# Linear-attention and MLP layers on one core: layer 1 started with ten TensorE-transposed tiles, another load order, biases by rows, and six sums off VectorE

## The chip, the cores and the metric

The kernel runs on one NeuronCore of a Trainium2 chip. Its engines work side by side, each through its own instruction queue in order: TensorE (PE in the profile, with its weight loads as PEld), VectorE (DVE), ScalarE (ACT), GpSimd (POOL) and SyncE (SP), which here only issues DMAs. The metric is the device time of one execution in microseconds; lower is better. What is reported is the median of several executions.

## The reference

Four layers act in turn on x, 2048 tokens by 576 channels, in bfloat16: A, B, A, B with the same weights for both A and both B.

```
x = x + A(layernorm(x));  x = x + B(layernorm(x));  x = x + A(layernorm(x));  x = x + B(layernorm(x))

A(x): q, k, v = x @ wqkv, 32 heads of 18;  phi(t) = where(t > 0, t + 1, exp(t)) + 1e-6
      kv = phi(k)^T v  and  z = sum phi(k), over all tokens
      o  = phi(q) kv / (phi(q) z + 1e-6);   return o @ wo
B(x): y = layernorm(x);  h = gelu_tanh(y @ w1 + b1), 4608 wide;  return h @ w2 + b2
```

Linear attention needs kv, the sum over all tokens, before any output of the layer; so layer A has two passes over the tokens.

## The kernel before

Tokens are cut into 16 tiles of 128. Everything stays on chip: x in `x_sb`, its normalised transpose in `yT` (channels on partitions, 5 blocks of 128 with the last one half filled), and all weights, each loaded once.

**Layer A, first pass** (`layer_A`, the loop at line 375). For each tile: `k_proj` (10 matmuls into two `k_ps` banks, exp on ScalarE, then phi finished on VectorE into `pk`), `v_proj` (10 matmuls, copied to `v_ring` by ScalarE), `kv_acc` of the tile before (5 matmuls that add to `kvacc`), and from tile 4 on one `q_proj` (`q_next`), which makes phi(q) for one group of heads and 512 tokens. There are 20 of these. **Second pass** (line 432): `num_stage` (5 matmuls, reciprocal and product on VectorE into a `y_ring` buffer, and a DMA transpose into `yT`, line 411) runs three tiles ahead of `wo_stage` (10 matmuls, and the residual sum). The residual sum of a tile is one VectorE instruction (line 305), but for tiles 4 to 7 it is a ScalarE copy (line 302) and a GpSimd sum (line 303). What is left of the 20 `q_proj` goes in between. After tiles 8, 10, 12 and 14 one group of the next MLP's first block is put in (`m1_group`, 36 matmuls), out of nine groups.

**The norm of a tile** (`Norm`) is four steps: statistics on VectorE (lines 211 to 220), the power -1/2 on GpSimd (line 225), the scaling on one of three engines (lines 236 and 240), and the transpose: either a DMA transpose issued by SyncE (line 249), or five TensorE transposes (line 253) and one copy of all five by ScalarE (line 255). In layer 1 the tiles 0 to 5 are transposed by TensorE, 6 to 15 by DMA; tiles 0 and 1 are scaled on VectorE and the others on GpSimd. Norms for later layers go through `Queue`: each `tick` lets every tile in it take its next step. In the second pass of layer A the first four tiles are fed to it for the MLP, scaled on ScalarE, their 64 tail channels doubled by GpSimd (line 244), and transposed by DMA.

**Layer B** (`LayerB`) takes blocks of 512 tokens: `m1_group` fills hT with gelu, then 72 matmuls for each tile and the residual sum. The lines 484 and 493 are its gelu and a one-column copy that orders its matmuls.

**What sets the order.** TensorE's order is written out: each matmul and transpose is chained to the one before (`pe`, line 122). The first loads are chained too (`chained`), all on SyncE's queue. The other engines get their order from a scheduler that runs when the kernel is built, by its own estimate of when things are ready; on the chip each engine keeps that order, so an instruction that waits holds back all behind it.

The loads of layer 1 are issued as follows: x tiles 0 and 1, k weights, x 2 and 3, v weights, x 4 and 5, then ten DMAs for the q weights, then two x tiles at the start of each tile of the first pass, and from tile 2 on one item of `late_pieces` in each: `wo`, nine pieces of `w1` (each with two small DMAs for its last 64 rows, `w1_tail`), the biases, and twelve pieces of `w2`. The bias b1 is read element by element into 128 partitions by 36 columns (`b1_raw`, line 171) and cast into `b1T` on VectorE (line 589).

Of the kernel before, what the change touches and what calls it, by code (L numbers as in the profile page):

```python
# [16 lines left out]
P = 128  # L17
NT = S // P
KD = 5
# [17 lines left out]
def build(tc, A_x, A_wqkv, A_wo, B_w1, B_b1, B_w2, B_b2, out, n_layers=4):  # L37
    nc = tc.nc
    with ExitStack() as ctx:
# [19 lines left out]
        def one(name):  # L59
            return ps_one.tile([P, 512], F32, name=name, tag="one")  # L60

# [80 lines left out]
        def load_wq(k):  # L142
            rows = P if k < 4 else 64
            src = A_wqkv[k * P:k * P + rows, :]
            chained(nc.sync.dma_start(out=wq_sb[0:rows, k, 0:4, 0:126],
                                      in_=src[:, 0:504].rearrange("p (g c) -> p g c", g=4)))
            chained(nc.sync.dma_start(out=wq_sb[0:rows, k, 4, 0:72], in_=src[:, 504:576]))
# [5 lines left out]
        def piece_w1(i):  # L153
            cs = slice(i * 512, (i + 1) * 512)
            chained(nc.sync.dma_start(out=w1_sb[:, 0:4, cs], in_=B_w1[0:4 * P, cs].rearrange("(k p) n -> p k n", p=P)))
            ts = slice(i * 256, (i + 1) * 256)
            for par in range(2):
                chained(nc.sync.dma_start(
                    out=w1_tail[64 * par:64 * (par + 1), ts].rearrange("k (f p) -> k f p", p=P),
                    in_=B_w1[4 * P:D, cs].rearrange("k (f two p) -> k f two p", two=2, p=P)[:, :, par, :]))  # L160
# [7 lines left out]
        def piece_biases():  # L168
            b1_raw = work.tile([P, NF], BF16, name="b1_raw", bufs=1)
            with nc.allow_non_contiguous_dma(reason="tiny one-time bias transpose load"):  # L170
                chained(nc.sync.dma_start(out=b1_raw[:], in_=B_b1.rearrange("(f p) -> p f", p=P)))
            bias_stage["b1"] = b1_raw
            chained(nc.sync.dma_start(out=b2_bc[:], in_=B_b2.partition_broadcast(P)))

# [28 lines left out]
        class Norm:  # L203
# [42 lines left out]
            def transposed(self):  # L246
# [3 lines left out]
                else:  # L250
                    tp = ps_one.tile([P, KD, P], BF16, name="tp", tag="one")
# [7 lines left out]
        class Queue:  # L259
# [3 lines left out]
            def feed(self, t, kind, eng="dve"):  # L263
                n = Norm(t, kind, eng, "dma")
# [44 lines left out]
        def layer_A(li, next_kind, before_tile, transposes, mlp):  # L309
# [65 lines left out]
            for t in range(NT):  # L375
                before_tile(t)
                k_proj(t)
                if t + 2 in transposes:
                    transposes[t + 2]()
# [3 lines left out]
                if t >= 4:  # L383
                    q_next()
            q_next()
# [263 lines left out]
```

## Time and profile before

| | us |
|---|---|
| median of 3 executions | 797.74 (797.67 to 798.62) |
| the profiled execution, its own time | 798.14 |
| its span, first to last instruction | 796.4 |
| TensorE busy in it | 765.2 |
| VectorE / ScalarE / GpSimd busy | 222.7 / 302.5 / 132.8 |
| mean granted TensorE clock | 0.987 |

A matmul row of the profile reads: line, engine, operation, what it writes and reads, shapes, count, and in brackets how long the engine had stood idle before it and who released it. All matmuls have line 129, the helper `mm`, so they are told apart by the tile they write: `k_ps`, `v_ps`, `kvacc`, `q_ps`, `num_ps`, `wo_ps` for layer A, `h_ps`, `hp_ps` and `m_ps` for layer B; `tp` (line 253) is the transpose. In the chain of waits a matmul's duration is its share of the pipelined stream, in the timeline it runs to its modelled end, so the latter is longer. "PEclk" is the TensorE clock that was granted, as a share of full speed.

### The profile page before, as it was taken

To read this page: it belongs to the slowest core of one execution; us is meant where nothing else is said; L and a number is where in the kernel's file an instruction comes from. 1 tells how busy PE (TensorE), PEld (TensorE's weight loads), DVE (VectorE), ACT (ScalarE), POOL (GpSimd) and SP (SyncE) were. 2 spreads that over 40 slices of the span, in tenths; PEclk is the share of its full clock that TensorE was granted. 3 is DMA by queue.
4 is the path that set the end of the run, shared out by engine and by line. 5 is a ranking of instruction groups with operands and counts; after the bars stand their busy time and mean duration, and the time that the engine had idled before them with its cause. 6 is when DMAs were issued, how large, how long until landed. Compare 5 with 4: busy or idle time off the path is not lost.

```text
span 796.4 us, 15153 instructions
## 1 busy us (share of the span) xinstructions
PE 765.2 (96%) x6416; PEld 488.8 (61%) x6416; DVE 222.7 (28%) x672; ACT 302.5 (38%) x638; POOL 132.8 (17%) x181
## 2 busy tenths in 40 slices
PE   7897979999999999999999996999999999999998
PEld 4675545477467547745787754546754774675476
DVE  6643884023103301300244576840000000000000
ACT  3464643600740461065036663343047016404610
POOL 7960060012102200200100004320100110010000
PEclk9998999999999999999999998999999999999999
DMA  8799153001300200100000015430000000000000
GB/s 212 187 206 274 39 104 59 2 9 17 43 1 17 51 2 9 17 10 1 18 17 1 1 34 93 84 58 8 16 9 1 16 16 1 2 23 9 2 8 23
DMA packets 86932, 33.88 MB, mean 43 GB/s; under 512 B 71696, under 2 KB 86864, under 8 KB 86864
## 3 DMA queue, kind: packets, MB, share of 16 engines
q1 hardware_dynamic: 86864, 32.91, 19.2%
q8 instruction: 50, 0.82, 0.4%
q14 instruction: 18, 0.15, 0.1%
HBM read 15.79 MB, written 2.36 MB: 23 GB/s over the span
## 4 chain that ended last, share of the span: by engine, by line
PE 83%; DVE 5%; POOL 4%; DMA 3%; issue 2%; ACT 1%; SPq 1%; POOLq 0%; DVEq 0%; ACTq 0%
PE m_ps L129 36%; PE h_ps L129 19%; PE hp_ps L129 15%; PE v_ps L129 4%; PE k_ps L129 4%; PE q_ps L129 3%; POOL y_ring L240 3%; DMA yT<-y_ring 2%; PE wo_ps L129 2%; DVE y_ring L408 1%; POOL ln_rstd L225 1%; PE kvacc L129 1%; DVE ln_st L211 1%; DMA b_raw<-in_B_b_dram 1%; DVE x_sb L305 1%
## 5 line engine op out<-in xcount | busy, mean ns | idle before, releaser
L129 PE MATMUL m_ps<-w_sb,hT 128*128 128x288 bf16 x2304 | 283.6, 286 | 0.0
L129 PEld LDWEIGHTS <-hT 128*128 128x128 bf16 x2304 | 224.8, 98 | 59.8 <-issue 3.4
L129 PEld LDWEIGHTS <-w_sb 64*128 64x128 bf16 x2304 | 123.9, 94 | 138.6 <-issue 4.6
L129 PE MATMUL hp_ps<-yT,w_sb 64*128 64x512 bf16 x1152 | 176.8, 376 | 0.8 <-DVE x_sb L305 0.8
L305 DVE TENSOR_TENSOR x_sb<-m_ps,xo 128x576 bf16<-128x576 f32 x32 | 24.2, 758 | 457.1 <-PE m_ps L129 457.1
L129 PE MATMUL h_ps<-yT,w_sb 64*128 64x512 bf16 x1152 | 149.2, 376 | 0.6 <-DVE y_ring L408 0.6
L493 ACT COPY relay_sb<-relay_sb 128x1 f32<-128x1 f32 x144 | 28.4, 197 | 283.2 <-PE h_ps L129 238.5
L129 PEld LDWEIGHTS <-yT 128*128 128x128 bf16 x960 | 94.1, 101 | 50.2 <-issue 10.7
L295 POOL TENSOR_TENSOR xo<-x_sb,b_bc 128x576 f32<-128x576 bf16 x32 | 40.8, 1274 | 456.1 <-DVE x_sb L305 455.8
L484 ACT ACTIVATE hT<-h_ps,b1T 128x512 bf16<-128x512 f32 x144 | 91.2, 684 | 44.5 <-PE h_ps L129 44.5
L484 ACT ACTIVATE hT<-hp_ps,b1T 128x512 bf16<-128x512 f32 x144 | 91.2, 693 | 0.0
L225 POOL TENSOR_TENSOR ln_rstd<-ln_u,neg_half 128x1 f32<-128x1 f32 x64 | 35.1, 552 | 148.9 <-DVE ln_u L220 127.4
L129 PE MATMUL wo_ps<-wo_sb,yT 128*128 128x288 bf16 x320 | 47.4, 298 | 9.4 <-DMA yT<-y_ring 9.2
L211 DVE BATCH_NORM_STATS2 ln_st<-x_sb 128x6 f32<-128x288 bf16 x128 | 52.3, 439 | 7.3 <-DMA x_sb<-in_A_x_dram 6.7
L129 PE MATMUL h_ps<-yT,w_tail 64*128 64x512 bf16 x144 | 54.1, 376 | 0.0
L129 PE MATMUL hp_ps<-yT,w_tail 64*128 64x512 bf16 x144 | 54.1, 376 | 0.0
L129 PE MATMUL k_ps<-wkv_sb,yT 128*128 128x288 bf16 x320 | 45.9, 290 | 8.0 <-DVE pk L328 7.7
L129 PE MATMUL q_ps<-yT,wq_sb 128*128 128x512 bf16 x200 | 50.3, 386 | 1.4 <-DVE y_ring L408 1.4
L129 PE MATMUL v_ps<-wkv_sb,yT 128*128 128x288 bf16 x320 | 47.6, 299 | 0.0
L323 ACT ACTIVATE phi_e<-k_ps 128x288 bf16<-128x288 f32 x64 | 24.4, 418 | 45.1 <-PE k_ps L129 42.1
L129 PEld LDWEIGHTS <-w_tail 64*128 64x128 bf16 x288 | 27.1, 94 | 17.1
L363 ACT ACTIVATE phi_e<-q_ps 128x512 bf16<-128x512 f32 x40 | 23.8, 596 | 26.8 <-PE q_ps L129 24.5
(59 smaller groups left out, 378.9 us busy)
## 6 DMA issues: line engine op xcount, KB each, us to landing
w_sb<-in_B_w_dram SPq DMA_DIRECT2D x12, 432.0 KB, 8.7
w_sb<-in_B_w_dram SPq DMA_DIRECT2D x9, 512.0 KB, 4.6
x_sb<-in_A_x_dram SPq DMA_DIRECT2D x16, 144.0 KB, 3.4
out_dram<-x_sb SPq DMA_DIRECT2D x16, 144.0 KB, 1.8
yT<-y_ring SPq DMA_TRANSPOSE x90, 2.6
wkv_sb<-in_A_wqkv_dram SPq DMA_DIRECT2D x2, 576.0 KB, 5.6
wo_sb<-in_A_wo_dram SPq DMA_DIRECT2D x1, 576.0 KB, 6.1
w_tail<-in_B_w_dram SPq DMA_DIRECT2D x18, 32.0 KB, 4.0
```

Source lines behind the costliest of these rows:

```text
L129: return pe(nc.tensor.matmul(out_, lhsT=lhsT, rhs=rhs, start=start, stop=stop, **kw))
L211: ins = nc.vector.bn_stats(out=stt[:, h, :], in_=xt[:, h * HALF:(h + 1) * HALF])
L225: nc.gpsimd.tensor_tensor(out=self.r[:], in0=self.u[:], in1=neg_half[:], op=ALU.pow)
L240: ins = eng.tensor_scalar(out=y[:, 0:D], in0=xt, scalar1=self.mv[:, 0:1], scalar2=self.r[:, 0:1], op0=ALU.subtract, op1=ALU.mult)
L295: nc.gpsimd.tensor_tensor(out=xo[:], in0=x_sb[:, t, :], in1=b2_bc[:], op=ALU.add)
L305: nc.vector.tensor_tensor(out=two(x_sb[:, t, :]), in0=halves, in1=two(xo), op=ALU.add)
L323: nc.scalar.activation(out=e[:, cols], in_=kp[:, 0:HALF], func=ACT.Exp)
L363: last["exp"] = nc.scalar.activation(out=e[:, 0:CA], in_=qp[:], func=ACT.Exp).ins.name
L408: nc.vector.tensor_tensor(out=o[:, h0 * DH:h1 * DH].rearrange("p (h c) -> p h c", c=DH), in0=nd[:, :, 0:DH], in1=rden[:, h0:h1].unsqueeze( ...
L484: last["gelu"] = nc.scalar.activation(out=hT[f][:, 0:CB], in_=dst[n], func=ACT.Gelu_apprx_tanh, bias=b1T[:, f:f + 1], scale=1.0).ins.name
L493: relay = nc.scalar.copy(out=relay_sb[:, 1:2], in_=relay_sb[:, 0:1])
```

## The change

1. Layer 1: the tiles transposed by TensorE are 0 to 9 (`TE = 10`), not 0 to 5; tile 2 is scaled on VectorE too; the transposes of tile t+2 stand at the end of tile t in TensorE's order, not between its k and v matmuls.
2. x tiles 6 to 9 are loaded ahead of the q weights and 10 to 15 right behind them; the q weights take seven DMAs, not ten.
3. `w1_tail` is loaded by two DMAs, not eighteen. The last four tiles of the first pass issue up to four late pieces each, so that all are issued there.
4. b1 is loaded as 36 rows of 128, transposed by TensorE after the last tile's `q_next`, and cast from PSUM.
5. The first `q_proj` stands at tile 3 in layer 1 and at tile 2 in layer 3, not at tile 4.
6. In both layers A the four tiles normalised for the MLP are transposed by TensorE and copied by ScalarE.
7. The residual sums of tiles 4 to 9, not 4 to 7, go by ScalarE and GpSimd.
8. The gelu table is loaded after tile 3 of the second pass, not 5, and MLP groups are put in after tiles 7, 9, 11, 13 and 15: five of them, not four.

```diff
@@ -59,6 +59,9 @@
         def one(name):
             return ps_one.tile([P, 512], F32, name=name, tag="one")
 
+        def one_bf16(name, shape):
+            return ps_one.tile(shape, BF16, name=name, tag="one")
+
 
         ident = const.tile([P, P], BF16, name="ident")
         nc.gpsimd.memset(ident[:], 0.0)
@@ -139,12 +142,14 @@
                                       in_=A_wqkv[0:4 * P, src].rearrange("(k p) n -> p k n", p=P)))
             chained(nc.sync.dma_start(out=wkv_sb[0:64, 4, dst], in_=A_wqkv[4 * P:D, src]))
 
-        def load_wq(k):
-            rows = P if k < 4 else 64
-            src = A_wqkv[k * P:k * P + rows, :]
-            chained(nc.sync.dma_start(out=wq_sb[0:rows, k, 0:4, 0:126],
-                                      in_=src[:, 0:504].rearrange("p (g c) -> p g c", g=4)))
-            chained(nc.sync.dma_start(out=wq_sb[0:rows, k, 4, 0:72], in_=src[:, 504:576]))
+        def load_wq():
+            for k in range(KD):
+                rows = P if k < 4 else 64
+                chained(nc.sync.dma_start(out=wq_sb[0:rows, k, 0:4, 0:126],
+                                          in_=A_wqkv[k * P:k * P + rows, 0:504].rearrange("p (g c) -> p g c", g=4)))
+            chained(nc.sync.dma_start(out=wq_sb[:, 0:4, 4, 0:72],
+                                      in_=A_wqkv[0:4 * P, 504:D].rearrange("(k p) c -> p k c", p=P)))
+            chained(nc.sync.dma_start(out=wq_sb[0:64, 4, 4, 0:72], in_=A_wqkv[4 * P:D, 504:D]))
 
         def piece_wo():
             chained(nc.sync.dma_start(out=wo_sb[:, 0:4, :], in_=A_wo[0:4 * P, :].rearrange("(k p) n -> p k n", p=P)))
@@ -153,11 +158,11 @@
         def piece_w1(i):
             cs = slice(i * 512, (i + 1) * 512)
             chained(nc.sync.dma_start(out=w1_sb[:, 0:4, cs], in_=B_w1[0:4 * P, cs].rearrange("(k p) n -> p k n", p=P)))
-            ts = slice(i * 256, (i + 1) * 256)
-            for par in range(2):
-                chained(nc.sync.dma_start(
-                    out=w1_tail[64 * par:64 * (par + 1), ts].rearrange("k (f p) -> k f p", p=P),
-                    in_=B_w1[4 * P:D, cs].rearrange("k (f two p) -> k f two p", two=2, p=P)[:, :, par, :]))
+
+        def piece_tail(par):
+            chained(nc.sync.dma_start(
+                out=w1_tail[64 * par:64 * (par + 1), :].rearrange("k (f p) -> k f p", p=P),
+                in_=B_w1[4 * P:D, :].rearrange("k (f two p) -> k f two p", two=2, p=P)[:, :, par, :]))
 
         def piece_w2(i):
             chained(nc.sync.dma_start(out=w2_sb[:, 3 * i:3 * (i + 1), :],
@@ -165,12 +170,19 @@
 
         bias_stage = {}
 
-        def piece_biases():
-            b1_raw = work.tile([P, NF], BF16, name="b1_raw", bufs=1)
-            with nc.allow_non_contiguous_dma(reason="tiny one-time bias transpose load"):
-                chained(nc.sync.dma_start(out=b1_raw[:], in_=B_b1.rearrange("(f p) -> p f", p=P)))
-            bias_stage["b1"] = b1_raw
+        def piece_b1():
+            rows = work.tile([NF, P], BF16, name="b1_rows", bufs=1)
+            chained(nc.sync.dma_start(out=rows[:], in_=B_b1.rearrange("(f p) -> f p", p=P)))
+            bias_stage["b1"] = rows
+
+        def piece_b2():
             chained(nc.sync.dma_start(out=b2_bc[:], in_=B_b2.partition_broadcast(P)))
+
+        def transpose_b1():
+            rows = bias_stage.pop("b1")
+            tp = one_bf16("b1_ps", [P, NF])
+            pe(nc.tensor.transpose(out=tp[:], in_=rows[:], identity=ident[0:NF, 0:NF]))
+            nc.vector.tensor_copy(out=b1T[:], in_=tp[:])
 
         load_x(0)
         load_x(1)
@@ -248,7 +260,7 @@
                 if self.transpose == "dma":
                     nc.sync.dma_start_transpose(out=yT[:, :, tok], in_=self.y[:])
                 else:
-                    tp = ps_one.tile([P, KD, P], BF16, name="tp", tag="one")
+                    tp = one_bf16("tp", [P, KD, P])
                     for k in range(KD):
                         pe(nc.tensor.transpose(out=tp[:, k, :], in_=self.y[:, k * P:(k + 1) * P], identity=ident[:]))
                     if self.transpose == "act":
@@ -260,8 +272,8 @@
             def __init__(self):
                 self.items = []
 
-            def feed(self, t, kind, eng="dve"):
-                n = Norm(t, kind, eng, "dma")
+            def feed(self, t, kind, eng="dve", transpose="dma"):
+                n = Norm(t, kind, eng, transpose)
                 self.items.append([n.stats, n.rstd, n.norm, n.transposed])
 
             def tick(self):
@@ -306,7 +318,7 @@
             if li == n_layers - 1:
                 nc.sync.dma_start(out=out_f[t * P:(t + 1) * P, :], in_=x_sb[:, t, :])
 
-        def layer_A(li, next_kind, before_tile, transposes, mlp):
+        def layer_A(li, next_kind, before_tile, after_tile, first_q, mlp):
             kvacc = pair("kvacc", "accA")
             pks, vas, pq = {}, {}, {}
 
@@ -375,13 +387,12 @@
             for t in range(NT):
                 before_tile(t)
                 k_proj(t)
-                if t + 2 in transposes:
-                    transposes[t + 2]()
                 v_proj(t)
                 if t >= 1:
                     kv_acc(t - 1)
-                if t >= 4:
+                if t >= first_q:
                     q_next()
+                after_tile(t)
             q_next()
             kv_acc(NT - 1)
             for bank, lo, heads, rows in ((0, 0, 3, 126), (1, 3, 1, 126), (1, 4, 1, 72)):
@@ -417,9 +428,9 @@
                     for k in range(KD):
                         mm(wp[:, half, 0:HALF], yT[:, k, tok], wo_sb[:, k, half * HALF:(half + 1) * HALF],
                            k == 0, k == KD - 1)
-                residual(li, t, wp[:, :, 0:HALF], on_pool=TPC <= t < 2 * TPC)
+                residual(li, t, wp[:, :, 0:HALF], on_pool=4 <= t < 10)
                 if next_kind == "B" and t < TPC:
-                    lnq.feed(t, "B", "act")
+                    lnq.feed(t, "B", "act", "act")
 
             q_next()
             q_next()
@@ -435,10 +446,10 @@
                 wo_stage(t)
                 q_next()
                 lnq.tick()
-                if t == 5:
+                if t == 3:
                     warm_table(ACT.Gelu_apprx_tanh, last["exp"])
-                if mlp is not None and t in (8, 10, 12, 14):
-                    mlp.m1_group(0, (t - 8) // 2)
+                if mlp is not None and t >= 7 and t % 2 == 1:
+                    mlp.m1_group(0, (t - 7) // 2)
                     mlp.flush()
 
         GF = 4
@@ -549,30 +560,32 @@
         kinds = ["A", "B", "A", "B"][:n_layers]
 
 
-        TE = 6
-        norms = [Norm(t, "A", "dve" if t < 2 else "pool", "act" if t < TE else "dma", after=(t if t >= 2 else None))
+        TE = 10
+        norms = [Norm(t, "A", "dve" if t < 3 else "pool", "act" if t < TE else "dma", after=(t if t >= 2 else None))
                  for t in range(NT)]
-        late_pieces = [piece_wo] + [(lambda i=i: piece_w1(i)) for i in range(9)] + [piece_biases] + \
+        late_pieces = [piece_wo, lambda: piece_w1(0), lambda: piece_w1(1), lambda: piece_tail(0), lambda: piece_tail(1)] + \
+                      [(lambda i=i: piece_w1(i)) for i in range(2, 9)] + [piece_b1, piece_b2] + \
                       [(lambda i=i: piece_w2(i)) for i in range(12)]
 
-        for t in range(2):
-            norms[t].stats()
-        for t in range(2):
-            norms[t].rstd()
+        norms[0].stats()
+        norms[0].rstd()
+        norms[1].stats()
+        norms[1].rstd()
         norms[0].norm()
         norms[0].transposed()
         norms[1].norm()
+        norms[1].transposed()
         for t in (2, 3):
             norms[t].stats()
             norms[t].rstd()
-        norms[1].transposed()
         norms[2].norm()
-        for k in range(KD):
-            load_wq(k)
+        for t in range(6, 10):
+            load_x(t)
+        load_wq()
+        for t in range(10, NT):
+            load_x(t)
 
         def before_tile0(t):
-            for u in range(6 + 2 * t, min(NT, 8 + 2 * t)):
-                load_x(u)
             if t + 4 < NT:
                 norms[t + 4].stats()
                 norms[t + 4].rstd()
@@ -581,21 +594,26 @@
                 if t + 3 >= TE:
                     norms[t + 3].transposed()
             if t >= 2:
-                for _ in range(2 if t == NT - 1 else 1):
-                    late_pieces.pop(0)()
+                for _ in range(1 if t < NT - 4 else 4):
+                    if late_pieces:
+                        late_pieces.pop(0)()
             if t == 8:
                 build_masks(last["pool_norm"])
+
+        def after_tile0(t):
+            if 2 <= t + 2 < TE:
+                norms[t + 2].transposed()
             if t == NT - 1:
-                nc.vector.tensor_copy(out=b1T[:], in_=bias_stage.pop("b1")[:])
+                transpose_b1()
 
         mlps = {li: LayerB(li, kinds[li + 1] if li + 1 < n_layers else None)
                 for li, kind in enumerate(kinds) if kind == "B"}
         for li, kind in enumerate(kinds):
             nk = kinds[li + 1] if li + 1 < n_layers else None
             if kind == "A" and li == 0:
-                layer_A(li, nk, before_tile0, {t: norms[t].transposed for t in range(2, TE)}, mlps.get(li + 1))
+                layer_A(li, nk, before_tile0, after_tile0, 3, mlps.get(li + 1))
             elif kind == "A":
-                layer_A(li, nk, lambda t: lnq.tick(), {}, mlps.get(li + 1))
+                layer_A(li, nk, lambda t: lnq.tick(), lambda t: None, 2, mlps.get(li + 1))
             else:
                 mlps[li].run()
         lnq.drain()
```

## The prediction

> **What bounds the kernel now.** I read the page's busy times and its DMA slices (40 of 19.9 us) first, to see whether there is room at all:
>
> ```profile
> PE 765.2 (96%) x6416; PEld 488.8 (61%) x6416; DVE 222.7 (28%) x672; ACT 302.5 (38%) x638; POOL 132.8 (17%) x181
> DMA  8799153001300200100000015430000000000000
> ```
>
> TensorE is the bound, and 31.2 us of the span (796.4 - 765.2) are all that idling costs; the change works in the two layers A, up to 119 us and from 406 to 525. A busy share hides cold matmuls, so second I cut them by what happens in them; the columns are stretch, length, busy time of the five engines, granted clock, DMA share, GB/s:
>
> ```profile
> 7.74:16.90 9.16, 6.08 (x40) 4.27 (x41) 5.02 (x20) 3.19 (x7) 7.37 (x6) 0.81 0.82 193
> 16.90:28.20 11.30, 11.30 (x108) 9.11 (x106) 10.28 (x40) 7.12 (x14) 10.88 (x9) 1.00 0.57 153
> 28.20:38.00 9.80, 6.43 (x36) 4.01 (x35) 4.08 (x16) 3.60 (x8) 9.49 (x7) 0.83 0.95 232
> 60.20:71.00 10.80, 6.47 (x32) 3.98 (x31) 3.61 (x11) 2.55 (x5) 0.00 (x0) 0.68 0.98 240
> 7.74:83.76 76.02, 65.24 (x485) 46.39 (x486) 39.14 (x128) 37.51 (x78) 42.23 (x33) 0.91 0.87 208
> 83.76:119.02 35.26, 29.69 (x241) 18.39 (x238) 30.20 (x107) 18.64 (x32) 13.45 (x23) 1.00 0.41 80
> 463.73:503.08 39.35, 32.18 (x239) 20.15 (x238) 30.40 (x106) 18.43 (x32) 13.48 (x23) 0.91 0.43 72
> ```
>
> The first pass of layer 1 (7.74 to 83.76) idles 76.02 - 65.24 = 10.78 us, all of it in three stretches (3.08, 3.37 and 4.33 us), and behind each idle the granted clock is low. The second pass up to the ninth output tile idles 5.57 us in layer 1 and 7.17 in layer 3. Third, who caused it: TensorE's waits, then the rows behind them (chain, VectorE, SyncE, GpSimd).
>
> ```profile
> PE wo_ps L129 <- DMA yT<-y_ring: 9.2, 6, 3.3
> PE k_ps L129 <- DVE pk L328: 7.7, 3, 4.3
> PE tp L253 <- POOL y_ring L240: 3.1, 1, 3.1
> ```
>
> The "pk" waits are VectorE standing still: at 30.87 it waits for an x tile, issued behind a DMA transpose, and at 63.59 for the bias, whose 9 KB take 6.07 us, so that the cast in front of it holds back pk.
>
> ```profile
> L211 DVE BATCH_NORM_STATS2 ln_st<-x_sb 128x6 f32<-128x288 bf16 x128 | 52.3, 439 | 7.3 <-DMA x_sb<-in_A_x_dram 6.7
> 30.87 0.46 DVE L211 BATCH_NORM_STATS2 ln_st<-x_sb 128x6 f32<-128x288 bf16 x1 [2.82 <-DMA x_sb<-in_A_x_dram]
> 57.49 6.07 DMA b_raw<-in_B_b_dram
> 63.59 0.18 DVE b1T L589
> 71.14 1.23 PE k_ps L129 x10
> 73.59 0.28 PE kvacc L129 x5
> 73.87 1.08 PE q_ps L129 x5
> 12.22 0.60 PE tp L253 x5
> 19.80 0.28 PE tp L253 x5
> 9.86 2.30 POOL L240 TENSOR_SCALAR y_ring<-x_sb,ln_mv,ln_rstd 128x576 bf16<-128x576 bf16 x1
> 12.80 2.37 POOL L240 TENSOR_SCALAR y_ring<-x_sb,ln_mv,ln_rstd 128x576 bf16<-128x576 bf16 x1
> 47.99 4.60 POOL L240 TENSOR_SCALAR y_ring<-x_sb,ln_mv,ln_rstd 128x576 bf16<-128x576 bf16 x2
> 4.35 0.52 SPq L140 DMA_DIRECT2D wkv_sb<-in_A_wqkv_dram  x1
> wkv_sb<-in_A_wqkv_dram SPq DMA_DIRECT2D x2, 576.0 KB, 5.6
> 83.28 0.29 DVE L365 TENSOR_SCALAR phi_e<-phi_e 128x512 bf16<-128x512 bf16 x1 [1.48 <-ACT phi_e L363]
> 83.77 0.42 DVE L367 TENSOR_TENSOR pq<-phi_a,phi_e 128x512 bf16<-128x512 bf16 x1 [0.19 <-ACT phi_a L364]
> ```
>
> **The change part by part: first pass of layer 1 (edits 1 to 5).** Warm, one tile costs 1.23 for k, as much for v and 0.28 for kvacc, 2.74 us, a q 1.08, a tile's five transposes 0.28. Before: 16 x 2.74 + 13 x 1.08 + 4 x 0.28 (tiles 2 to 5; 0 and 1 come before 7.74) = 59.0 of the 76.02 us. So 17.0 are lost: 10.8 idle and 6.2 cold. After: one q more (+1.08), four tiles' transposes more (+1.12) and the bias transpose (at most 0.28): 61.5 us of warm work. What becomes of the three stalls:
>
> - The 3.1 us wait for GpSimd's first scaling (9.86) goes: tile 2 is scaled on VectorE, and GpSimd starts with tile 3. What is late next are the v weights. Their issue at 4.35 is unchanged and a load of this kind lands in 5.6 us, near 10.1, while k ends near 9.0 (7.74 + 1.23): I take 1.2, between 0 and the 3.1 of before.
> - The wait at 30.87 goes: all x tiles are issued ahead of any transpose. The q weights slip behind four x tiles (4 x 147 KB, 2.8 us at the 208 GB/s of this pass) and are wanted no earlier than the third tile's end near 20; they were all issued by 13.3 before.
> - The wait at 63.59 goes: 36 rows of 256 bytes in place of 4608 single elements. The cover is distance: in SyncE's order the bias stands behind the last DMA transpose (tile 15, whose scaling ended at 52.6, the second of the two at 47.99) and two w1 pieces, some 52 us, landing near 58; TensorE reaches its transpose near 69. If this cover goes, TensorE itself waits there.
>
> GpSimd now has 13 tiles, not 14, at 2.94 us each (12.80 - 9.86). Tile 3 is ready near 13, tile t 2.94 (t - 3) later, tile 15 near 50 with the masks; TensorE comes to them at about 14.4 and then at 3.0 to 4.1 us a tile, so it stays behind GpSimd after tile 3. ScalarE gets four copies more and is busy 37.5 of 76: hidden. SyncE loses 4 transposes, 16 tail issues and 3 q issues; nobody waits for the later weights before the MLP. I add 1.5 us for VectorE's order around the early x tiles (its statistics waited 6.7 us for x tiles, 2.82 of them at 30.87; TensorE did not feel the other 3.9, and may now). Sum: 76.02 - 61.5 - 1.2 - 1.5 = **11.8 us gained**. Bounds: 14.5 with neither residue; 5 where a stall like the third stays (4.33 idle and 2.6 cold).
>
> **Second pass of layer 1 (edits 6 to 8).** Its limit is VectorE (30.20 busy of 35.26), then SyncE's order. The rows of output tile 7 (and the matmul of tile 8), with layer 3's below:
>
> ```profile
> 105.07 0.81 DVE L408 TENSOR_TENSOR y_ring<-num_ps,rden 128x378 bf16<-128x378 f32 x2
> 105.58 1.21 SPq L249 DMA_TRANSPOSE yT<-y_ring  x1
> 106.84 1.28 SPq L411 DMA_TRANSPOSE yT<-y_ring  x1
> 109.54 1.40 PE L129 MATMUL wo_ps<-wo_sb,yT 128*128 128x288 bf16 x10 [1.24 <-DMA yT<-y_ring]
> 112.18 1.40 PE L129 MATMUL wo_ps<-wo_sb,yT 128*128 128x288 bf16 x10 [0.96 <-DMA yT<-y_ring]
> 485.00 0.81 DVE L408 TENSOR_TENSOR y_ring<-num_ps,rden 128x378 bf16<-128x378 f32 x2
> 488.26 1.20 SPq L249 DMA_TRANSPOSE yT<-y_ring  x1
> 489.52 1.27 SPq L411 DMA_TRANSPOSE yT<-y_ring  x1
> 493.09 2.07 PE L129 MATMUL wo_ps<-wo_sb,yT 128*128 128x288 bf16 x10 [3.34 <-DMA yT<-y_ring]
> 488.00 0.24 POOL L244 COPY y_ring<-y_ring 128x64 bf16<-128x64 bf16 x1
> 490.07 0.24 POOL L244 COPY y_ring<-y_ring 128x64 bf16<-128x64 bf16 x1 [0.96 <-ACT y_ring L236]
> 488.08 1.39 PE L129 MATMUL wo_ps<-wo_sb,yT 128*128 128x288 bf16 x10
> ```
>
> The data was there at 105.88 but SyncE was busy with a norm transpose until 106.8. That goes: 0.96 us. VectorE has one q less in this stretch, 0.72 us (0.29 + 0.42, and an issue gap). The wait of tile 8 behind it, 0.96 us, falls under an MLP group, which now comes after tile 7. Together 2.6; I take **2.5**. Tiles 8 and 9 leave VectorE, at a time when TensorE runs without gaps: 0. The gelu table is loaded behind the last exp, before as after: 0. The fifth MLP group only moves. The four transposes (1.12 us) lie in TensorE's idle time; if that is gone they cost 1.1. Bounds 0 and 4.
>
> **Layer 3 (edits 5 to 8).** Two q move into the first pass, where TensorE has no gap: +2.16 there. In the second pass the same SyncE order costs more: data ready at 485.81, but at the queue's head a norm transpose waits until 488.26 for GpSimd's tail copy; the output's own goes at 489.52, and TensorE idles 3.34 us, then runs cold (2.07 us for a 1.23 us tile). This stretch takes 39.35 us, layer 1's 35.26. Without the norm transposes and two q (1.44 us of VectorE) the data is ready at 484.4, lands within 2.6 to 4.1 us, and wo 7 runs near 488 instead of 493. With the cold matmuls (0.84 here, some 1.2 in the two groups behind) the stretch loses 7.1 us. Net 7.1 - 2.16 = **4.9 us**, bounds 1 and 7.
>
> Here the change adds a wait: TensorE's transpose stands in order behind wo 3 to 6, and all its work queues behind it. Layer 3's tail copies ended at 488.24 and 490.31, wo 5 and 6 at 488.0 and 489.5: waits of 0.3 and 0.8 us, with the first two tiles early. VectorE's shorter list brings both forward; I keep 0.4 inside the 7.1.
>
> **The sum.** 11.8 + 2.5 + 4.9 = 19.2 us. Against the profiled execution's 798.14: 778.9. The median of the runs is 0.4 lower, so **778.5 us**.
>
> One rule speaks against it. The Trainium skill, "TensorE: Matmul & The Clock Gate", Part 4, gives about 275 ns for a 128x128 transpose inside a kernel and says that transposes do not count as activity for the clock. By its figure an estimate for the twelve added tiles is 60 x (275 - 56) ns = 13 us more, 792 in all. The trace disagrees: five take 0.28 us in the chain, and the stretch 16.90 to 28.20, which holds three of these groups, ran at a granted clock of 1.00.
>
> **The rivals.** (a) *A stall stays in the first pass.* VectorE's order is made by a scheduler's estimate, and both pk stalls came from an estimate that was too early; x 6 to 15 now come closer together. For: VectorE's four waits for x, 6.7 us in all. Against: x no longer queues behind a transpose. Price: 4.33 idle and 2.6 cold come back, so 785.5. (b) *Weights push the output transposes.* All w2 pieces now issue in the first pass, which ends near 72; DMA was full until 80 before. If the stream still ended at 80, the first output would land at 82.6 instead of 79, and the next ones after it: 3.6 to 6 us, so 783. Against: the stream lost the bias's six slow microseconds. (c) *Slower, by one mechanism:* TensorE waits at its eight new transposes for GpSimd, which now has six sums of 1.28 us there instead of four. It decides against the change if each of the eight waits reaches 2.6 us (20.8 / 8), which takes two sums ahead of every tail copy; then 800. Against: the waits of before, had the transposes stood there, were 0 to 0.8. (d) *Transposes dearer in their new places:* after a gap five took 0.60, not 0.28; for twelve tiles 3.8 us, or with the skill's figure the 792 above. (e) *It doesn't do what it says:* the gaps are filled elsewhere by equal ones, so 797.5. (f) *Better:* no residue in the first pass and the upper bounds of the rest: 772.
>
> **How the numbers follow.** My forecast, 774 to 784, 0.57; (a) 0.20; (b) 0.06; (c) 0.06; (d) 0.03; (e) 0.02; (f) 0.06. The time is that of the forecast. The range 771 to 789 leaves out (c), (e), half of (d) and the far end of (a). A measurement of this kernel can tell about 0.2% (1.6 us) from no change; by that, faster 0.92, same 0.02, slower 0.06.
>
> **What would show it.** Right: the last kvacc of layer 1 ends near 72 instead of 83.8, with no TensorE wait over 2 us in between and a granted clock of 1.00 past 20 us; no wait on the bias; layer 3's stretch from the last kvacc to the ninth output tile near 32 us; only output transposes on SyncE there. Wrong: a wait of tp for GpSimd over 1 us in the second passes, a new k_ps wait on pk, or wo waits on DMA still above 6 us in total.

## The result and the profile after

The changed kernel takes 789.23 us (median of 4 executions, 788.58 to 791.46), the kernel before, run beside it, 797.75 (797.67 to 798.62): a ratio of 0.990, 95% interval 0.988 to 0.992. So it is faster by 8.5 us where 19.2 were forecast, and the time lies 0.2 us above the range. The profiled execution is the longest of the four: 791.46 us, span 789.8, against 798.14 and 796.4 before. (Of one experiment below, e4, the profiled execution was disturbed and took 2056 us; its profile and that time aren't used.)

The page's busy times and DMA slices after:

```profile
PE 762.9 (97%) x6461; PEld 490.5 (62%) x6477; DVE 221.1 (28%) x659; ACT 311.1 (39%) x654; POOL 133.2 (17%) x180
DMA  8688242001201300000000014430000000000000
```

The edits give TensorE 61 more instructions (PEld, its weight loads, counts 6477 against 6416; 16 of the matmul records of q are missing after, so PE shows only 45 more), and it is busy 2.3 us less, so some of its matmuls ran faster. 26.9 us of idling are left (789.8 - 762.9), 4.3 less than before. The waits of TensorE after (the main ones: total, times, longest):

```profile
PE k_ps L132 <- DVE pk L340: 9.0, 4, 5.2
PE num_ps L132 <- ACT yT L267: 5.2, 5, 1.8
PE hp_ps L132 <- DVE x_sb L317: 2.0, 1, 2.0
PE tp L265 <- POOL ln_rstd L237: 1.4, 1, 1.4
PE wo_ps L132 <- DMA yT<-y_ring: 1.2, 1, 1.2
```

The 9.2 us that wo waited for DMA transposes are down to 1.2, and the 3.1 us for GpSimd's first scaling are gone. But k waits for pk 9.0 us in all, where it was 7.7: the two waits named in the prediction are gone and others stand in their place. The stretches after (columns as in the prediction: the whole first pass of layer 1, two parts of it, then the second passes of layers 1 and 3 up to output tile 9, counted from 0, with one MLP group in each):

```profile
7.74:83.15 75.41, 66.00 (x505) 47.30 (x513) 42.10 (x132) 40.46 (x84) 39.20 (x32) 0.93 0.76 201
31.00:42.94 11.94, 6.83 (x35) 4.36 (x36) 4.13 (x12) 2.87 (x7) 11.84 (x15) 0.71 0.44 112
42.94:83.15 40.21, 39.94 (x320) 28.85 (x323) 21.04 (x53) 26.25 (x56) 7.24 (x4) 1.00 0.79 220
83.15:115.71 32.56, 28.94 (x253) 19.00 (x252) 28.97 (x103) 20.44 (x35) 11.68 (x21) 1.00 0.32 62
462.57:494.99 32.42, 27.71 (x249) 18.63 (x247) 27.54 (x100) 19.37 (x33) 11.54 (x21) 1.00 0.38 57
```

Both second passes came out near the size forecast: 35.26 became 32.56 (2.7 less) and 39.35 became 32.42 (6.9 less, 7.1 forecast). The first pass hardly moved: 76.02 became 75.41. From 42.94 on it runs with 0.3 us of idling at full clock; all the loss is ahead of that, and more than half of the idling (5.11 of 9.41 us) lies between 31.00 and 42.94, where TensorE works 6.83 of 11.94 us at a granted clock of 0.71. In that stretch GpSimd is busy without a pause, 11.84 of 11.94.

TensorE's timeline after, at its stops in the first pass (start, duration, what, and in brackets the idle time before it and who ended it):

```profile
14.04 0.77 PE L132 MATMUL k_ps<-wkv_sb,yT 128*128 128x288 bf16 x5 [1.08 <-DVE pk L340]
...
26.65 1.39 PE L132 MATMUL k_ps<-wkv_sb,yT 128*128 128x288 bf16 x10 [2.45 <-DVE pk L340]
...
36.05 2.56 PE L132 MATMUL k_ps<-wkv_sb,yT 128*128 128x288 bf16 x10 [5.16 <-DVE pk L340]
38.41 2.60 PE L132 MATMUL v_ps<-wkv_sb,yT 128*128 128x288 bf16 x10
```

Behind the stop of 5.16 us ten matmuls take 2.56 and 2.60 us instead of 1.39; up to 42.94 the cold ones cost 2.8 us. What VectorE did ahead of the two late pk (its timeline after, where L230 is the step of a tile's norm that hands the variance, `ln_u`, to GpSimd):

```profile
26.00 0.15 DVE L230 TENSOR_SCALAR ln_u<-ln_mv 128x1 f32<-128x1 f32 x1 [1.40 <-POOL ln_rstd L237]
...
26.19 0.77 DVE L340 SCALAR_TENSOR_TENSOR pk<-k_ps,phi_e 128x288 bf16<-128x288 f32 x2
...
35.07 0.15 DVE L230 TENSOR_SCALAR ln_u<-ln_mv 128x1 f32<-128x1 f32 x1 [2.64 <-POOL ln_rstd L237]
...
35.54 0.82 DVE L340 SCALAR_TENSOR_TENSOR pk<-k_ps,phi_e 128x288 bf16<-128x288 f32 x2
```

and GpSimd's timeline after at the last of these:

```profile
29.00 2.31 POOL L252 TENSOR_SCALAR y_ring<-x_sb,ln_mv,ln_rstd 128x576 bf16<-128x576 bf16 x1
31.28 0.56 POOL L237 TENSOR_TENSOR ln_rstd<-ln_u,neg_half 128x1 f32<-128x1 f32 x1
31.94 2.57 POOL L252 TENSOR_SCALAR y_ring<-x_sb,ln_mv,ln_rstd 128x576 bf16<-128x576 bf16 x1
34.48 1.58 POOL L237 TENSOR_TENSOR ln_rstd<-ln_u,neg_half 128x1 f32<-128x1 f32 x3
```

VectorE wants to write `ln_u` of a tile and waits for the end of GpSimd's power of an earlier one. The reason is in the code: `ln_u` is a ring of four buffers, so tile t+4 can be written when the power of tile t has read its place. GpSimd makes a power and a scaling in turn, about 2.9 us a tile, and the power of a tile stands behind the scaling of the tile before. In VectorE's order the statistics of all 16 tiles stand ahead of pk of the fifth tile (tile 4), so the pk of tiles 3 and 4 (26.19 and 35.54) stand behind five waits for GpSimd's power, 8.8 us in all, two ahead of the first and three ahead of the second (VectorE's waits after, between 20 and 36):

```profile
DVE ln_u L230 <- POOL ln_rstd L237: 8.8, 5, 2.6
```

The stop of 1.08 us at 14.04 isn't one of these: no such wait stands ahead of its pk.

Before, VectorE's order held the same trap one tile later; there VectorE first stood for an x tile, and then 2.64 us in the same way, which reached TensorE as a wait of 0.63 us (VectorE's timeline before):

```profile
36.65 0.15 DVE L218 TENSOR_SCALAR ln_u<-ln_mv 128x1 f32<-128x1 f32 x1 [2.64 <-POOL ln_rstd L225]
```

### The profile page after: what moved, and what is told of

The parts are those of the page before. It is cut to its first block, busy times and chain, and to the rows that moved or that the text cites. A ratio compares the mean times of both kernels' runs of the same rounds, so it can differ in the third digit from the quotient of the medians.

```text
span 789.8 us, 15212 instructions
## 1 busy us (share of the span) xinstructions
PE 762.9 (97%) x6461; PEld 490.5 (62%) x6477; DVE 221.1 (28%) x659; ACT 311.1 (39%) x654; POOL 133.2 (17%) x180
## 5 line engine op out<-in xcount | busy, mean ns | idle before, releaser
L223 DVE BATCH_NORM_STATS2 ln_st<-x_sb 128x6 f32<-128x288 bf16 x124 | 50.3, 439 | 4.8 <-POOL x_sb L315 2.7
L132 PE MATMUL q_ps<-yT,wq_sb 128*128 128x512 bf16 x184 | 46.8, 380 | 2.3 <-DVE y_ring L419 1.5
L132 PE MATMUL v_ps<-wkv_sb,yT 128*128 128x288 bf16 x320 | 46.0, 292 | 0.0
L132 PE MATMUL wo_ps<-wo_sb,yT 128*128 128x288 bf16 x320 | 44.1, 286 | 1.3 <-DMA yT<-y_ring 1.2
```

The lines of the kernel that those rows point to most:

```text
L132: return pe(nc.tensor.matmul(out_, lhsT=lhsT, rhs=rhs, start=start, stop=stop, **kw))
L223: ins = nc.vector.bn_stats(out=stt[:, h, :], in_=xt[:, h * HALF:(h + 1) * HALF])
```

## The experiments

The theory after the comparison: the ring of four places holds VectorE to GpSimd's pace while the statistics are ordered early (T1). Its rivals: the new load order (T2), the GpSimd chain itself being too slow for the first pass (T3), and for the smaller second-pass gain, q moved or transposes moved. Each run was compared with the kernel before on the same chip (797.77, 797.31 and 796.89 us in the three groups e1 to e4, e5 to e8, e9 to e12).

**e1: more places.** The changed kernel with 16 buffers in all three rings of the norm; every engine keeps its order.

```diff
-                self.mv = work.tile([P, 2], F32, name="ln_mv", bufs=6)
-                self.u = work.tile([P, 1], F32, name="ln_u", bufs=4)
-                self.r = work.tile([P, 1], F32, name="ln_rstd", bufs=6)
+                self.mv = work.tile([P, 2], F32, name="ln_mv", bufs=16)
+                self.u = work.tile([P, 1], F32, name="ln_u", bufs=16)
+                self.r = work.tile([P, 1], F32, name="ln_rstd", bufs=16)
```

> The changed kernel with one edit: the three small norm buffers ln_u, ln_mv and ln_rstd have 16 places each (4, 6 and 6 before), so that no tile's statistics wait for an older tile's power or scaling on GpSimd. The order of instructions on every engine is unchanged. Theory R (the first pass of layer 1 stalls because VectorE writes ln_u of tile t+4 into the place that GpSimd's power of tile t still has to read, with pk behind it): VectorE's waits on ln_rstd between 20 and 36 us vanish, TensorE's waits of 2.45 and 5.16 us and the cold stretch of about 3 us behind them go, the last kvacc of layer 1 ends at 72 to 75 instead of 83, and the time is 778 to 782. Rival L (the early x loads and the DMA traffic, or GpSimd's rate of 2.9 us a tile itself, hold the pass): the waits move to another cause and the time stays within 3 us of 789.

Measured: 778.52 us (778.11 to 778.74), ratio 0.976 (0.974 to 0.978): 10.7 below the changed kernel. TensorE's waits and its first pass in e1:

```profile
PE k_ps L132 <- DVE pk L340: 1.8, 2, 1.5
PE v_ps L132 <- DMA wkv_sb<-in_A_wqkv_dram: 1.1, 1, 1.1
```

```profile
7.75:72.35 64.60, 61.34 (x505) 45.24 (x513) 42.19 (x132) 40.06 (x84) 39.45 (x32) 1.00 0.86 230
```

The same 505 recorded matmuls and transposes take 61.34 us instead of 66.00, at full clock, and the pass ends 10.8 us earlier. The two stops of 2.45 and 5.16 us and the 2.8 us of cold matmuls are 10.4 of that. The stop at 14 us stays (1.45 in e1): it isn't the ring's. GpSimd does the same work in the same order, so T3 falls.

**e2: which ring.** Only `ln_u` gets 16 buffers.

```diff
-                self.u = work.tile([P, 1], F32, name="ln_u", bufs=4)
+                self.u = work.tile([P, 1], F32, name="ln_u", bufs=16)
```

> The changed kernel with only ln_u at 16 places; ln_mv stays at 6. Theory R, finer: the place of ln_mv of tile t+6 is free after the scaling of tile t, some 3.7 us earlier than the place of ln_u would be, so most of the stall goes but not all: 780 to 786, between the run with all three rings and the changed kernel. Rival L: within 3 us of 789.

Measured: 784.32 us (783.14 to 786.67), ratio 0.984 (0.981 to 0.986): 4.9 of e1's 10.7, as expected. TensorE's wait for pk fell from 9.0 to 5.6 us, 1.8 of which e1 has too:

```profile
PE k_ps L132 <- DVE pk L340: 5.6, 4, 2.4
```

With one ring longer the next short one holds VectorE: the mean and variance, `ln_mv`, with six places, whose reader is GpSimd's scaling (VectorE's waits in e2, between 20 and 40):

```profile
DVE ln_mv L227 <- POOL y_ring L252: 5.1, 3, 2.1
```

**e3: the order.** The rings stay short, but each tile's statistics are ordered behind the pk that precedes them in the program.

```diff
                     if self.after is not None:
                         tc.add_manual_dep(ins.ins, last["dve_norm"], NOSYNC, reason="first tiles go first")
+                        if phi_last["last"] is not None:
+                            tc.add_manual_dep(ins.ins, phi_last["last"], NOSYNC, reason="statistics behind phi")
...
-                    nc.vector.scalar_tensor_tensor(out=pk[:, cols], in0=kps[half][:, 0:HALF], scalar=0.0, in1=e[:, cols],
-                                                   op0=ALU.max, op1=ALU.add)
+                    ins = nc.vector.scalar_tensor_tensor(out=pk[:, cols], in0=kps[half][:, 0:HALF], scalar=0.0,
+                                                         in1=e[:, cols], op0=ALU.max, op1=ALU.add)
+                    phi_last["last"] = ins.ins.name
```

> The changed kernel with its rings as they are, but each tile's statistics ordered on VectorE behind the pk of the tile before in program order, so that they can't run ahead of the work that TensorE waits for. Theory R: an in-order engine can't be held by a place that is not yet free if the writer comes later; the stalls on pk go as well, 778 to 784. If instead the small rings matter by themselves, 786 or more.

Measured: 777.16 us (777.05 to 777.25), ratio 0.974 (0.972 to 0.976), 12.1 below the changed kernel. The first pass in e3, and the wait for pk:

```profile
7.74:70.42 62.68, 61.17 (x505) 45.26 (x512) 43.74 (x132) 40.06 (x84) 40.09 (x32) 1.00 0.94 241
```

```profile
PE k_ps L133 <- DVE pk L343: 0.4, 1, 0.4
```

The pass is 1.9 us shorter than in e1, because the order also shortens the stop near 14 us, 1.45 in e1, to 0.39 and others by less.

**e9: both cures together.** e3 and e1 in one kernel.

> The changed kernel with both cures, the statistics behind pk and 16 places in the norm rings. If both cures remove the same wait, it adds nothing to the order alone: 776 to 778.5, against 777.2. If the two remove different waits: 774 or less.

Measured: 777.02 us (776.67 to 777.21), ratio 0.975 (0.973 to 0.976), 0.1 from e3. Two cures of one wait don't add up: what e1 removes is part of what e3 removes.

**e8: the load order of before.** The changed kernel with two x tiles issued in each tile of the first pass and the q weights ahead of them, as before.

```diff
-        for t in range(6, 10):
-            load_x(t)
         load_wq()
-        for t in range(10, NT):
-            load_x(t)
...
         def before_tile0(t):
+            for u in range(6 + 2 * t, min(NT, 8 + 2 * t)):
+                load_x(u)
```

> The changed kernel with the x loads and q weights where they were before (q weights first, then two x tiles at the start of each tile), all else as changed. Theory R (the small rings and the order on VectorE): the statistics still run ahead, the stalls on pk stay, 786 to 791. Rival L (loading all x early is what lets the statistics run ahead): the stalls shrink, 784 or less.

Measured: 788.20 us (788.11 to 789.85), ratio 0.990 (0.988 to 0.993), the same as with the new order to within the executions' spread. The stop is there, and longer (TensorE's timeline in e8):

```profile
35.13 2.56 PE L132 MATMUL k_ps<-wkv_sb,yT 128*128 128x288 bf16 x10 [6.55 <-DVE pk L340]
```

T2 falls: the stop doesn't need the new load order, and while VectorE is held by the ring, loading x earlier or later changes the time by less than the spread.

**e6: the order alone on the kernel before.** The edit of e3, with the same lines as there, made in the kernel before, nothing else.

> The kernel before with the statistics of a tile ordered on VectorE behind the pk of the tile before, and nothing else. If the same run-ahead of the statistics held the kernel before (its waits of 2.73 and 0.63 us on pk near 31 and 37, and the cold matmuls behind them), these go and the bias wait of 4.33 us stays: 791 to 794. If those waits were the late x loads themselves: 796 to 798.

Measured: 796.50 us (793.92 to 796.88), ratio 0.999 (0.997 to 1.000). A miss: next to nothing came out of it. VectorE's and TensorE's timelines in e6 tell why:

```profile
62.03 0.18 DVE L593 CAST b1T<-b_raw 128x36 f32<-128x36 bf16 x1 [9.39 <-DMA b_raw<-in_B_b_dram]
```

```profile
64.15 1.36 PE L130 MATMUL k_ps<-wkv_sb,yT 128*128 128x288 bf16 x5 [7.05 <-DVE pk L331]
```

The bias lands at 62.0 here and at 63.6 before, and the pk of the last five tiles stand behind its cast. Time saved ahead of it is spent waiting for it: 7.05 us in place of the 4.33 of before.

**e7: the order and the bias by rows.** e6 with edit 4 of the change.

```diff
-                chained(nc.sync.dma_start(out=b1_raw[:], in_=B_b1.rearrange("(f p) -> p f", p=P)))
+            rows = work.tile([NF, P], BF16, name="b1_rows", bufs=1)
+            chained(nc.sync.dma_start(out=rows[:], in_=B_b1.rearrange("(f p) -> f p", p=P)))
...
+            if li == 0:
+                transpose_b1()
             q_next()
             kv_acc(NT - 1)
```

> The run before, and the bias loaded by rows and transposed by TensorE. The wait of 4.33 us at 61 and the 2.6 us of cold matmuls behind it go too: 6 to 7 us below the run with the order alone, 785 to 787. If the bias wait only uncovers another wait of the same length, within 2 us of it.

Measured: 786.66 us (785.73 to 787.80), ratio 0.988 (0.986 to 0.990): 9.8 below e6. That is the wait of 7.05 us and the cold matmuls behind it. These two edits on the kernel before give 10.7 us, 2 more than all eight edits of the change without the order. TensorE's two largest waits in e7:

```profile
PE wo_ps L130 <- DMA yT<-y_ring: 9.0, 7, 2.4
PE tp L261 <- POOL y_ring L248: 3.5, 1, 3.5
```

They are waits that the change's other edits are made for: after it, wo waits 1.2 us and tp for GpSimd's scaling not at all.

**e4: the second passes alone.** The kernel before with edits 6, 7 and 8.

```diff
-                n = Norm(t, kind, eng, "dma")
+                n = Norm(t, kind, eng, transpose)
...
-                residual(li, t, wp[:, :, 0:HALF], on_pool=TPC <= t < 2 * TPC)
+                residual(li, t, wp[:, :, 0:HALF], on_pool=4 <= t < 10)
                 if next_kind == "B" and t < TPC:
-                    lnq.feed(t, "B", "act")
+                    lnq.feed(t, "B", "act", "act")
...
-                if t == 5:
+                if t == 3:
                     warm_table(ACT.Gelu_apprx_tanh, last["exp"])
-                if mlp is not None and t in (8, 10, 12, 14):
-                    mlp.m1_group(0, (t - 8) // 2)
+                if mlp is not None and t >= 7 and t % 2 == 1:
+                    mlp.m1_group(0, (t - 7) // 2)
```

> The kernel before with the edits of the second passes alone (four norms a layer transposed by TensorE, six sums on ScalarE and GpSimd, MLP groups after tiles 7 to 15, the gelu table after tile 3); first passes and loads as before. If the second passes gave nearly all of the measured gain: 788 to 791. If the first pass of layer 1 gave half of it: 793 to 795.

Measured: 794.47 us (793.62 to 794.74), ratio 0.996 (0.994 to 0.997): 3.3 us, not nearly all of the change's gain.

**e5: and the q moved.** e4 with edit 5.

```diff
-                if t >= 4:
+                if t >= (3 if li == 0 else 2):
                     q_next()
```

> The kernel before with the second-pass edits and the earlier start of q_proj (tile 3 in layer 1, tile 2 in layer 3); loads, bias and the ten transposes as before. By the two traces the second passes gained 2.7 us in layer 1 and, after 2.3 us more in its first pass, 3.2 in layer 3; layer 1's first pass pays 1.1 for its extra q. So 793 (792 to 794), that is, more than half of the change's gain without its part 1 to 4. If moving q is what made the second passes shorter, it is below the run without it (794.5) by 1 us or more; if not, within 1 us of it.

Measured: 793.88 us (792.37 to 795.16), ratio 0.996 (0.995 to 0.998). That is within a microsecond of e4, which by the expectation speaks against the moved q as the cause of the shorter second passes. But e5's profile leaves it open, because layer 3, with the same edits, gains less here than in the changed kernel. From the last kvacc of layer 1 to the first k of layer 3 it gains the same 2.7 us; layer 3, from its first k to its last wo, takes 119.5 us (402.63 to 522.1), against 120.1 before and 116.9 in the changed kernel. There wo of tile 3 waits 1.93 us for a DMA transpose, and TensorE's clock is low behind it (stretch in e5):

```profile
477.11:486.28 9.17, 7.93 (x56) 6.03 (x56) 6.34 (x23) 3.72 (x6) 4.12 (x9) 0.63 0.25 47
```

Why the transpose comes late for TensorE here and not in the changed kernel stays open.

**e11: the norms' transposes back to SyncE.** e3 without edit 6.

```diff
-                    lnq.feed(t, "B", "act", "act")
+                    lnq.feed(t, "B", "act")
```

> The changed kernel with the statistics behind pk and the norms of the second passes transposed by DMA as before; six sums, MLP groups, q and all else as changed. If SyncE's queue, in which an output's transpose stands behind a waiting norm transpose, held the second passes: 780 to 784, with TensorE waits on wo for DMA of 5 us or more in total. If the moved MLP group and the shorter list of VectorE did it: within 1.5 us of 777.

Measured: 781.00 us (779.63 to 784.15), ratio 0.980 (0.978 to 0.983), 3.8 us above e3. TensorE's waits in e11:

```profile
PE wo_ps L133 <- DMA yT<-y_ring: 7.2, 6, 2.5
PE h_ps L133 <- DMA yT<-y_ring: 1.6, 1, 1.6
```

The waits come back with the norm transposes on SyncE, everything else as in e3. In the profiled execution (779.77) the second passes up to output tile 9, first of layer 1, then of layer 3, are:

```profile
71.05:105.46 34.41, 29.56 (x234) 18.99 (x232) 28.84 (x103) 18.19 (x31) 11.54 (x21) 0.95 0.40 78
452.33:485.92 33.59, 27.47 (x229) 17.47 (x227) 28.12 (x101) 17.20 (x29) 11.50 (x21) 1.00 0.46 81
```

e3 takes 32.56 and 32.58 there. So SyncE's order does hold the second passes: edit 6, with what its transposes cost on TensorE taken off, is worth 1.9 and 1.0 us in this execution. But in layer 3, with the norm transposes on SyncE as before, the stretch is still 5.8 us below the 39.35 of before. Which of the other edits gave that (the moved q, the six sums, the MLP groups) was not run one by one. Only this execution of e11 has a profile.

**e10: six tiles on TensorE.** e3 with `TE = 6`, so that tiles 6 to 9 are transposed by DMA again.

```diff
-        TE = 10
+        TE = 6
```

> The changed kernel with the statistics behind pk and six TensorE-transposed tiles in layer 1, not ten. By the prediction's step the DMA transposes of tiles 6 to 9 are hidden and the four on TensorE cost 1.1 us: 776 to 777. Rival: without the TensorE transposes the DMA ones stand in SyncE's queue behind weight loads and come late for k: 778.5 or more.

Measured: 779.91 us, but six executions lie between 776.28 and 781.43 (ratio 0.980, 0.978 to 0.982), where e3's lie within 0.2 us. The median is the rival's (778.5 or more), but its mechanism isn't seen: the profiled execution (777.38) shows no wait of k for a DMA. In it the first pass ends 0.8 us earlier than in e3 (last kvacc at 69.30, not 70.14), near the 1.1 expected for four tiles' transposes. So the four tiles cost TensorE about that, and with them the executions lie closer together; what varies without them isn't seen in one profile and stays open.

**e12: a seventh buffer.** e9 with seven `y_ring` buffers in place of six, for the waits of VectorE on buffers that a DMA transpose still reads.

```diff
-NY = 6
+NY = 7
...
+        nc.gpsimd.memset(y_ring[5][:], 0.0)
```

> The run with both cures and seven y_ring buffers, not six (the seventh cleared by GpSimd). If the wait of 1.6 to 2.0 us on a residual sum in layer 3 comes from VectorE waiting for a y_ring buffer that a DMA transpose still reads, that wait and the cold matmuls behind it shrink: 774 to 776. If not: within 1 us of the run with both cures.

Measured: 776.28 us (775.89 to 776.66), ratio 0.974 (0.972 to 0.975), 0.7 below e9 and 0.3 above the range expected. TensorE's wait for the residual sum, 1.4 us in e9, is 0.5:

```profile
PE hp_ps L133 <- DVE x_sb L321: 0.5, 1, 0.5
```

This is the fastest of all: 20.6 us below the kernel before of its group.

## Why the prediction was right or wrong

**First pass, forecast 11.8, measured 0.6 (83.76 to 83.15).** The step that failed is the last term of that sum: "I add 1.5 us for VectorE's order around the early x tiles". Its real size was 1.5 + 11.2 = 12.7 us. The other terms stood. In e1, where only the ring's wait is taken out, the warm work takes 61.34 us (61.5 forecast), the v weights cost 1.1 (1.2), and 2.2 are left for the term that was put at 1.5; the pass ends at 72.35, so 11.4 us are gained; in e3 13.3, inside the bounds of 5 to 14.5. The changed kernel itself lies outside these bounds, since the lower one was one stall of the size seen before.

Two readings led there. "The wait at 30.87 goes" was true of the row, but the row named only the last of two waits in one queue: with x there, VectorE ran on to the next, the four places of `ln_u`. The row at 36.65 of the profile before shows it; the prediction doesn't have it. And GpSimd's 2.94 us a tile was compared with TensorE's progress alone ("it stays behind GpSimd after tile 3"); that was right for TensorE, and VectorE, whose statistics run up to eleven tiles ahead, was tied to the same chain.

Rival (a), "a stall stays in the first pass", described the place and the kind (VectorE's order, "a new k_ps wait on pk" among the signs), and its 785.5 lies 3.7 us from the time; only the 792 of rival (d) lies nearer, for a price that isn't there (below). The mechanism of (a), x tiles coming late, wasn't the one (e8), and its price of 6.9 us was the old stall's: the two stops of 2.45 and 5.16 us and the cold matmuls behind the second cost 10.7 (e1).

**The bias.** Right: no wait for it after; SyncE issues the rows at 55.02 and TensorE transposes at 81.66. e6 and e7 show more than was forecast: as long as it lands near 62, almost no gain ahead of it counts (0.8 us in e6), and edit 4 is worth 9.8 us on the kernel before once the order is mended.

**Second pass of layer 1, forecast 2.5.** Measured 2.7 by the stretches, and 2.7 from the end of the last kvacc to the first k of layer 3 (322.3 before, 319.6 after). e11 bears out the step on SyncE's order: without edit 6 the stretch is 1.9 us longer than in e3.

**Layer 3, forecast 4.9, measured 3.3 in the profiled execution.** From its first k to its last wo (TensorE by tile, first and last start of each group, in microseconds) before and after:

```profile
L129 PE MATMUL k_ps<-wkv_sb,yT x160: 284/286/286, 406.1 to 459.7; 128*128 128x288 bf16 x160
L129 PE MATMUL wo_ps<-wo_sb,yT x160: 283/286/448, 471.6 to 526.2; 128*128 128x288 bf16 x160
```

```profile
L132 PE MATMUL k_ps<-wkv_sb,yT x160: 284/286/286, 402.7 to 458.5; 128*128 128x288 bf16 x160
L132 PE MATMUL wo_ps<-wo_sb,yT x160: 282/286/297, 470.4 to 519.6; 128*128 128x288 bf16 x160
```

120.1 became 116.9. The two q cost 2.16 us in the first pass (57.67 became 59.83), as forecast. In e1, whose layer 3 has the same edits, the layer takes 114.8 (391.9 to 506.7), so 5.4 gained, and 115.2 in e3. The difference lies in the end of the pass, the same work in both (stretches of after, then of e1):

```profile
494.99:508.00 13.01, 13.01 (x122) 7.29 (x121) 9.06 (x28) 6.24 (x13) 6.33 (x9) 1.00 0.52 89
508.00:519.80 11.80, 9.78 (x65) 4.90 (x64) 8.29 (x26) 2.92 (x6) 3.30 (x9) 0.86 0.44 85
```

```profile
484.14:497.15 13.01, 13.01 (x122) 7.27 (x121) 9.44 (x29) 6.25 (x13) 6.35 (x9) 1.00 0.48 88
497.15:506.90 9.75, 8.10 (x66) 4.37 (x63) 6.63 (x23) 2.80 (x6) 3.06 (x8) 1.00 0.43 84
```

After, TensorE stops 1.99 us for a residual sum there (the one such stop of before is 0.8 us) and is granted 0.86 of its clock in that stretch; in e1 it stops 1.55 us and keeps the full clock. The profiled execution, 2.2 us above its median, lost 2.05 there. That the other executions keep their clock there, as e1 does, fits their times but wasn't seen. The prediction doesn't have this wait. Its size for the layer was met where the clock held (e1, e3) and missed where it didn't (0.6 us in e5). And the step behind the size was right only in part: by e11 edit 6, which clears SyncE's queue, is worth 1.0 of the 6.9 us that the stretch in layer 3 gained. The forecast put its 7.1 down to that queue and to two q less, so that the size came out is partly luck; what gave the rest stays open.

**The whole.** 0.6 + 2.7 + 3.3 = 6.6 us, by which the two spans differ. With the ring's wait taken out, e1 gives 778.52, where 778.5 was forecast, and its own sum is 11.4 + 2.7 + 5.4 = 19.5, where 19.2 was forecast. So the sizes were right except for one term, which the forecast took to be about an eighth of what it was; of the steps behind them, the one for layer 3 holds only in part.

**The other rivals.** (b) didn't come: the output transposes land in time, wo waits 1.2 us in all. (c) didn't: in the second passes tp doesn't wait for GpSimd; 1.4 us are at the start of layer 1. Instead the added transposes brought a wait that the prediction doesn't have, num_ps for ScalarE's copy of them (5.2 us in five stops), which lies within what the stretches above still gained. (d) didn't: five transposes take 0.28 us in the stream also in their new places (TensorE's timeline of e1, from this start to the next):

```profile
16.08 0.44 PE L265 MATMUL tp<-ident,y_ring 128*128 128x128 bf16 x5
16.36 1.39 PE L132 MATMUL k_ps<-wkv_sb,yT 128*128 128x288 bf16 x10
```

The Trainium skill ("TensorE: Matmul & The Clock Gate", Part 4) gives about 275 ns for one. As the price of a transpose in the stream that doesn't show here: five take 0.28 us from start to start, while the record of one lasts 219 ns on average, because the records overlap. And the first pass of e1, which holds eight such groups, runs at a granted clock of 1.00 (the prediction's stretch, 16.90 to 28.20, holds two whole groups and the end of a third).

## What to carry to other kernels

When a wait is to be removed, read what stands behind it in the same queue, not only who waits for it: an in-order engine goes on to its next wait, and a wait that was short before, because a longer one stood ahead of it, can take the whole gain. A tiny buffer reused every few tiles ties the engine that writes it to the slowest engine that reads it; if a scheduler may move the writes early, give it as many places as tiles, or tie the writes to the work that they must not overtake. And a transfer that lands at a fixed time eats all that is gained ahead of it (e6), so two such edits have to be tried together before either is judged.

## What the runs showed of the hardware

- The length of one stop doesn't tell whether a low clock follows. Behind a stop of 1.93 us the granted clock was 0.63 (e5), and with one of 1.99 us it was 0.86 in the 11.80 us around it (after); stops of 1.55 (e1) and 1.77 us (e3) left it at 1.00, and so did the one of 2.45 us that ended at 26.65 in the changed kernel:

```profile
26.65:30.73 4.08, 4.08 (x35) 3.02 (x35) 2.11 (x8) 1.49 (x4) 3.98 (x3) 1.00 0.54 72
```

  The Trainium skill ("TensorE: Matmul & The Clock Gate", Part 1, What's actually happening) puts the fall to the cold clock behind an idle window of about 3.4 us; the stops of 1.93 and 1.99 us were shorter. What decides it stays open. Behind 5.16 us of standing, ten matmuls took 2.56 us instead of 1.39.
- GpSimd's power of 128 numbers, one to a partition, takes 0.56 us (at 31.28 in the changed kernel), a quarter of the 2.31 us of its scaling of 128x576 (at 29.00).
